# A linear attention block whose engines' instruction lists are written straight behind the launch's beginning, without a block

## The chip, the core and the metric

The kernel runs on one core of one Trainium2 chip. The metric is the device time of one execution in microseconds (us); the time of a kernel is the median of its runs.

A core has five engines, each with an instruction list of its own: TensorE (PE; its weight loads are the row PEld), VectorE (DVE), ScalarE (ACT), GpSimd (POOL) and SyncE (SP, which here only issues transfers and waits). They are held together by semaphores alone. A name with a q at its end (SPq, PEldq) is the engine's sequencer: instructions that wait, branch, drain or issue a transfer, in which the engine itself does nothing.

## What is computed

```python
B, S, D = 1, 2048, 640;  H = 32; Dh = 20
q, k, v = split(x @ wqkv)                       # per head
phi = lambda t: where(t > 0, t + 1, exp(t)) + 1e-6
pq, pk = phi(q), phi(k)
kv  = einsum("bhsd,bhse->bhde", pk, v)          # 20 x 20 per head
z   = einsum("bhsd->bhd", pk)
num = einsum("bhqd,bhde->bhqe", pq, kv)
den = einsum("bhqd,bhd->bhq", pq, z)[..., None] + 1e-6
out = (num / den).reshape(B, S, D) @ wo
```

The inputs and the output are bf16: x is 2048 x 640, wqkv 640 x 1920, wo 640 x 640.

## The kernel before

The sequence of 2048 rows is cut into 16 tiles of 128 rows, and the width of 640 into five chunks of 128. TensorE first runs six matmuls on a constant (line 269) while the first x tiles and the K weights arrive, transposes the first x tiles itself (line 194), and then makes K for all 16 tiles (line 278). From K follow phi(k), the product of phi(k) with x in two halves of the width (line 305) and, between its steps, Q (line 331). Then come the denominators (line 454), the small per-head matrices (lines 408 and 432), and the output: each tile of 128 rows is multiplied with the folded weights (line 487), evicted from PSUM by ACT (line 509) and DVE (line 512) and stored by SP (line 497). The last tile is cut in three pieces, and its last store is issued by ACT.

The kernel does not call the engines while it lays out the work. A class `Plan` records every operation with the tiles that it reads and writes (`add`), works out from these which semaphores it must wait for, and keeps one list for each engine. Only at the end does `emit(engine, handle)` write a list out: for each operation its waits, the operation, and the increment of its semaphore. So the order on each engine is fixed before a single instruction is written, and the two ends of a list are set by where `emit` is called.

Before this point the launch (line 673, where the program object is made) has already written its own beginning: POOL sets four constants in memory, and all five engines meet at an opening barrier. In it every engine drains and adds one to a semaphore (gather); POOL waits until four have done so, takes the four off again, and adds four to a second semaphore (release), of which each other engine takes one.

Behind it the kernel opens a block (`nc.Block()`, line 636) and gives it a function for each engine: SP at lines 638 to 643, POOL 645, ACT 649, DVE 653, TensorE 657. The program then has seven parts: the beginning, one for each engine and an end. The beginning ends with an unconditional branch of each engine to its own part; each part ends with a branch to the end; and the end is a second, closing barrier of all five engines, built like the opening one. All of the closing part stands under line 95, where the stack of contexts is closed.

SP's list has something more behind its last operation: a wait for each of the 17 output stores (line 643), so that the program isn't over before its output has landed. The compiler puts two such waits into one instruction; the last of them it has folded into SP's closing branch.

Of the kernel before, what the change touches and what calls it, by code (L numbers as in the profile page):

```python
# [82 lines left out]
def bass_standalone__linear_attn_block__prompt_kernel(nc, x, wqkv, wo, out):  # L83
# [11 lines left out]
    with contextlib.ExitStack() as ctx:  # L95
        es = ctx.enter_context
# [35 lines left out]
        P = Plan(nc, es)  # L132
# [370 lines left out]
        out_keys = []  # L503
# [129 lines left out]
            out_tile(st, 2 * (st % 4) if st > 5 else 2 * (st % 2))  # L633
        out_last(NT - 1, (6, 7, 0))

        block = es(nc.Block())

        @block.sync
        def _(e):
            P.emit("sp", e)  # L640
            for key in out_keys:
                op = P.writers[key]
                e.wait_ge(P.sem_obj[op.sem], op.val)

        @block.gpsimd
        def _(e):
            P.emit("pool", e)

        @block.scalar
        def _(e):  # L650
            P.emit("act", e)

        @block.vector
        def _(e):
            P.emit("dve", e)

        @block.tensor
        def _(e):
            P.emit("pe", e)


# [26 lines left out]
```

## Time and profile before

| | us |
|---|---|
| median of 3 runs | 102.03 |
| the runs | 102.68, 102.03, 101.84 |
| the profiled execution | 102.49 |
| span of the profiled execution, first to last instruction | 100.6 |
| busy: PE, DVE, ACT, POOL | 97.1, 69.3, 43.3, 3.2 |

The span counts the opening and the closing barrier. The profiled execution's own time is 1.9 us longer than its span; what fills that is not in the trace. The granted TensorE clock is 1.000 of full speed throughout.

How to read it: a row of a source line gives the sequencer's or engine's instructions of that line, their number, the least, middle and largest duration in ns, and when the first and the last of them start, in us to one decimal. A row of the timeline gives start, duration, engine, line, operation, tiles, and in brackets how long the engine had been idle and what ended that. In a table of stretches each row is a part of the span with the busy time of each engine in it.

### The profile page before, as it was taken

The page shows a single profiled execution, that of the slowest core. Times are in us where ns is not written, and L with a number is a line of the kernel's source. Part 1 is how long each engine was busy: PE and PEld are TensorE (multiplying, and loading weights), DVE is VectorE, ACT ScalarE, POOL GpSimd, SP SyncE. Part 2 cuts the span into 40 slices and gives each one's busy share as a digit, 9 for nine tenths or more (in the row PEclk, how much of TensorE's full clock was granted, in tenths as well). Part 3 has the DMA queues.
Part 4 walks back from the last instruction along what each step waited for, and adds up shares of the span by engine and source line. Part 5 has one row for each costly group of instructions (what it writes and reads, how often), then busy time and mean ns, then how long its engine had stood idle before and what let it go on. Part 6 is the DMA issues. An engine that isn't in the chain of part 4 may idle for free.

```text
span 100.6 us, 1810 instructions
## 1 busy us (share of the span) xinstructions
PE 97.1 (97%) x703; PEld 63.2 (63%) x703; DVE 69.3 (69%) x140; ACT 43.3 (43%) x76; POOL 3.2 (3%) x15
## 2 busy tenths in 40 slices
PE   6999999999999999999999999999999999999990
PEld 2567777777777666656567565755537677777770
DVE  0217998888889378899996445668899669853331
ACT  5005554445697220462132228389844531333330
POOL 6600000000000000000000000000000000000000
PEclk9999999999999999999999999999999999999999
DMA  2954989999999400000000000114440323632233
GB/s 51 330 206 92 226 173 159 173 354 372 364 358 207 76 3 0 0 3 0 7 0 0 0 0 0 31 28 122 136 119 0 130 76 103 256 131 105 99 123 130
DMA packets 17076, 11.93 MB, mean 119 GB/s; under 512 B 8749, under 2 KB 17069, under 8 KB 17069
## 3 DMA queue, kind: packets, MB, share of 16 engines
q1 hardware_dynamic: 16349, 11.14, 39.8%
q10 hardware_dynamic: 720, 0.70, 2.0%
q8 instruction: 5, 0.08, 0.4%
q14 instruction: 2, 0.02, 0.1%
HBM read 5.90 MB, written 2.62 MB: 85 GB/s over the span
## 4 chain that ended last, share of the span: by engine, by line
PE 90%; DVE 4%; ACT 2%; issue 1%
PE ps L278 22%; PE ps L487 22%; PE ps L305 22%; PE ps L331 16%; PE ps L269 3%; DVE pq L344 2%; PE ps L194 2%; PE ps L408 2%; PE ps L454 1%; ACT eq L339 1%; DVE pq L479 1%; PE ps L432 1%; DVE eq L341 1%; ACT w2g L436 1%; DVE osb L512 0%
## 5 line engine op out<-in xcount | busy, mean ns | idle before, releaser
L331 PE MATMUL ps<-xT,wqp 128*128 128x512 bf16 x100 | 24.2, 379 | 0.0
L305 PE MATMUL ps<-pk,xn 128*128 128x320 bf16 x160 | 23.5, 300 | 0.0
L278 PE MATMUL ps<-wk,xT 128*128 128x320 bf16 x160 | 22.9, 304 | 0.0
L487 PE MATMUL ps<-w2p,pq 128*128 128x320 bf16 (+1 forms) x165 | 22.1, 295 | 0.1
L339 ACT ACTIVATE eq<-ps 128x512 bf16<-128x512 f32 x20 | 12.0, 599 | 21.2 <-PE ps L331 20.7
L305 PEld LDWEIGHTS ps<-pk,xn 128*128 128x128 bf16 x160 | 15.5, 98 | 7.5 <-DVE pt L320 0.2
L487 PEld LDWEIGHTS ps<-w2p,pq 128*128 128x128 bf16 x165 | 15.7, 98 | 6.7 <-DVE pq L479 0.6
L278 PEld LDWEIGHTS ps<-wk,xT 128*128 128x128 bf16 x160 | 15.6, 99 | 6.6 <-DVE xT L199 0.3
L291 ACT ACTIVATE ek<-ps 128x640 bf16<-128x640 f32 x16 | 11.2, 704 | 14.8 <-PE ps L278 14.8
L331 PEld LDWEIGHTS ps<-xT,wqp 128*128 128x128 bf16 x100 | 9.7, 97 | 9.0
L344 DVE SCALAR_TENSOR_TENSOR pq<-ps,eq 128x512 bf16<-128x512 f32 x20 | 13.8, 692 | 0.7
L296 DVE SCALAR_TENSOR_TENSOR pk<-ps,ek 128x640 bf16<-128x640 f32 x16 | 13.2, 825 | 0.6
L512 DVE CAST osb<-ps 128x320 bf16<-128x320 f32 (+1 forms) x16 | 7.7, 480 | 7.9 <-PE ps L487 7.8
L509 ACT CAST osb<-ps 128x320 bf16<-128x320 f32 (+1 forms) x17 | 7.0, 416 | 13.4 <-PE ps L487 11.5
L341 DVE TENSOR_SCALAR eq<-eq 128x512 bf16<-128x512 bf16 x20 | 5.8, 292 | 9.8 <-ACT eq L339 9.7
L479 DVE TENSOR_TENSOR pq<-pq,rd 128x512 bf16<-128x512 bf16 x20 | 7.8, 417 | 0.7 <-DMA rd<-rdc 0.7
L293 DVE TENSOR_SCALAR ek<-ek 128x640 bf16<-128x640 bf16 x16 | 5.2, 325 | 2.0 <-ACT ek L291 1.9
L199 DVE COPY xT<-ps 128x256 bf16<-128x256 bf16 (+1 forms) x8 | 2.2, 320 | 6.2 <-PE ps L194 6.2
L350 DVE TENSOR_TENSOR za<-pk 128x1280 f32<-128x1280 bf16 x4 | 5.8, 1482 | 0.0
L350 DVE TENSOR_TENSOR za<-za 128x1280 f32<-128x1280 f32 x3 | 4.4, 1481 | 0.0
L259 ACT COPY wqp<-wqn 128x640 bf16<-128x640 bf16 x5 | 4.3, 935 | 0.0
L436 ACT CAST w2g<-ps 120x640 bf16<-120x640 f32 (+1 forms) x6 | 4.0, 690 | 0.0
(38 smaller groups left out, 33.2 us busy)
## 6 DMA issues: line engine op xcount, KB each, us to landing
out_dram<-osb SPq DMA_DIRECT2D x15, 160.0 KB, 1.8
xn<-in_x_dram SPq DMA_DIRECT2D x3, 640.0 KB, 8.0
wqn<-in_wqkv_dram SPq DMA_DIRECT2D x1, 800.0 KB, 5.5
wv<-in_wqkv_dram SPq DMA_DIRECT2D x1, 800.0 KB, 11.3
wog<-in_wo_dram SPq DMA_DIRECT2D x1, 750.0 KB, 13.2
w2p<-w2g SPq DMA_DIRECT2D x5, 150.0 KB
rd<-rdc SPq DMA_DIRECT2D x8, 64.0 KB, 2.4
wk<-in_wqkv_dram SPq DMA_DIRECT2D x3, 160.0 KB, 4.1
```

What stands on the lines that cost most here:

```text
L278: r = e.matmul(bank(b + h, HALF), xT[:, c * S + 128 * st:c * S + 128 * st + 128], wk[:, c * D + HALF * h:c * D + HALF * (h + 1)], start=(c ...
L291: P.add("act", lambda e: e.activation(fold(t[:, :]), two_banks(b), ACTF.Exp), reads=banks + ["table"], writes=[("ek", st % 3)])
L296: P.add("dve", lambda e: e.scalar_tensor_tensor(fold(pk[:, st * D:(st + 1) * D]), two_banks(b), 0.0, fold(t[:, :]), ALU.max, ALU.add), rea ...
L305: r = e.matmul(bank(d, HALF), xn[:, st * D + 128 * d:st * D + 128 * d + 128], pk[:, st * D + HALF * h:st * D + HALF * (h + 1)], start=(st ...
L331: r = e.matmul(bank(b), wqp[:, d * D + 128 * c:d * D + 128 * c + 128], xT[:, d * S + BK * sbk:d * S + BK * (sbk + 1)], start=(d == 0), sto ...
L339: P.add("act", lambda e: e.activation(t[:, :], bank(b), ACTF.Exp), reads=[("bank", b), "table"], writes=[("eq", i)])
L344: P.add("dve", lambda e: e.scalar_tensor_tensor(pq[:, c * S + BK * sbk:c * S + BK * (sbk + 1)], bank(b), 0.0, t[:, :], ALU.max, ALU.add), ...
L350: P.add("dve", lambda e: e.tensor_tensor(d_ap, a, b, ALU.add), reads=ra + rb, writes=[dst])
L479: P.add("dve", lambda e: e.tensor_tensor(v, v, rd[i][:, BK * o:BK * (o + 1)], ALU.mult), reads=[("rd", i, 2 * o), ("rd", i, 2 * o + 1), (" ...
L487: r = e.matmul(bank(b, hi - lo), pq[:, c * S + 128 * st:c * S + 128 * st + 128], w2p[:, c * D + lo:c * D + hi], start=(c == 0), stop=(c == ...
L509: P.add("act", lambda e: e.copy(osb[j][:, lo:hi], bank(b, hi - lo)), reads=[("bank", b)], writes=keys)
L512: P.add("dve", lambda e: e.tensor_copy(osb[j][:, lo:hi], bank(b, hi - lo)), reads=[("bank", b)], writes=keys)
```

## The change

The block, its five functions, the branches into and out of it and its closing barrier are gone. The five lists are written one after the other straight into the program's beginning, behind the opening barrier, TensorE's first and SP's last; SP's waits for the output stores follow its list as before. The opening barrier stays.

```diff
-        block = es(nc.Block())
-
-        @block.sync
-        def _(e):
-            P.emit("sp", e)
-            for key in out_keys:
-                op = P.writers[key]
-                e.wait_ge(P.sem_obj[op.sem], op.val)
-
-        @block.gpsimd
-        def _(e):
-            P.emit("pool", e)
-
-        @block.scalar
-        def _(e):
-            P.emit("act", e)
-
-        @block.vector
-        def _(e):
-            P.emit("dve", e)
-
-        @block.tensor
-        def _(e):
-            P.emit("pe", e)
+        P.emit("pe", nc.tensor)
+        P.emit("act", nc.scalar)
+        P.emit("dve", nc.vector)
+        P.emit("pool", nc.gpsimd)
+        P.emit("sp", nc.sync)
+        for key in out_keys:
+            op = P.writers[key]
+            nc.sync.wait_ge(P.sem_obj[op.sem], op.val)
```

On each engine the instructions from the first tile operation to the last stand in the same order in both programs. Missing from the changed one are two branches on each of the five engines, and the closing barrier's drain and semaphore instructions. SP's waits for the stores are nine instructions now, where they were eight and a branch with a wait in it.

## The prediction

> **What bounds the kernel now.** I read the page's first two lines of busy time, then the chain of waits that ended last, then the first microsecond and the last two of the timeline, and last the single source lines at both ends, because the change touches nothing but the two ends.
>
> ```profile
> span 100.6 us, 1810 instructions
> PE 97.1 (97%) x703; PEld 63.2 (63%) x703; DVE 69.3 (69%) x140; ACT 43.3 (43%) x76; POOL 3.2 (3%) x15
> PE 90%; DVE 4%; ACT 2%; issue 1%
> ```
>
> TensorE carries the span: 97.1 of 100.6 us busy and 90% of the chain. The change adds, drops and moves none of its 703 matmuls and none of the other engines' tile work. So what it can do lies where TensorE is not working, and the table of busy time by stretches shows how little that is:
>
> ```profile
> core 0: us, PE busy (x) PEld busy (x) DVE busy (x) ACT busy (x) POOL busy (x), PEclk, DMA share, GB/s
> 0.00:0.80 0.80, 0.00 (x0) 0.00 (x0) 0.00 (x0) 0.00 (x0) 0.21 (x5) 1.00 0.00 0
> 0.80:98.20 97.40, 97.15 (x703) 63.18 (x703) 68.94 (x140) 43.32 (x76) 3.04 (x11) 1.00 0.43 119
> 98.20:98.60 0.40, 0.00 (x0) 0.00 (x0) 0.32 (x1) 0.00 (x0) 0.00 (x0) 1.00 0.97 362
> 98.60:100.20 1.60, 0.00 (x0) 0.00 (x0) 0.00 (x0) 0.00 (x0) 0.00 (x0) 1.00 0.36 111
> 100.20:100.60 0.40, 0.00 (x0) 0.00 (x0) 0.00 (x0) 0.00 (x0) 0.00 (x0) 1.00 0.00 0
> ```
>
> Five stretches: the launch's beginning (0.80 us), the work (97.40), the last eviction (0.40), the last stores on their way (1.60), and 0.40 us in which no engine works and no DMA moves a byte. The middle three stay. The first and the last are the change's.
>
> **The change part by part.**
>
> (a) *The opening branches.* Each engine's list begins with one unconditional branch in the program; the changed program has none. What does one cost? The tensor engine's branch is made at line 657, SP's at line 638.
>
> ```profile
> nothing on L657; most used: ['L487', 'L278', 'L305', 'L331', 'L79', 'L454', 'L408', 'L194', 'L432', 'L339', 'L341', 'L344', 'L390', 'L479', 'L673', 'L509', 'L497', 'L291', 'L293', 'L296', 'L512', 'L269', 'L95', 'L199', 'L471']
> L673 SPq EVENT_SEMAPHORE  x1: 17/17/17, 0.7 to 0.7; - x1
> L673 PEldq EVENT_SEMAPHORE  x1: 51/51/51, 0.7 to 0.7; - x1
> 0.80 0.40 SPq L220 DMA_DIRECT2D xn<-in_x_dram  x1
> 0.81 0.14 PEld L269 LDWEIGHTS ps<-const-bfloat16-1.0 128*128 128x128 bf16 x2 [0.81 <-issue]
> ```
>
> No opening branch leaves a record, and the first instruction stands at 0.80 or 0.81 us right behind the opening barrier's release, which starts at 0.7 (0.65 to 0.75 by the rounding) and lasts 17 to 51 ns. What could be a branch is at most the gap between: 0.80 - 0.65 - 0.02 = 0.13 us on SP, at least 0. A branch that goes to the very next instruction seems to have been dropped when the program was compiled. I take 0; 0.13 us is the other end. It would count in full, because the start sets when the first x tile lands and TensorE waits for it. The Trainium skill (Advanced Engine Details and Errata, Control Flow Timing) gives some 51 ns to a branch that is always taken; by that the sum below would be 0.05 us lower, and no run here shows such a branch.
>
> That start is the only place where the branches could be hidden by anything: six warm-up matmuls run from 0.84, and TensorE then waits for the x tile.
>
> ```profile
> 0.84 2.72 PE L269 MATMUL ps<-const-bfloat16-1.0 128*128 128x512 bf16 x6 [0.84 <-PEq L673]
> PEld ps L194 <- DMA xn<-in_x_dram: 0.9, 1, 0.9
> ```
>
> The transfer ends that wait, so an earlier TensorE start alone would bring nothing; only SP's earlier DMA would. With a price of 0 for SP's branch there is nothing to cover.
>
> (b) *The closing branches and the closing barrier.* They all stand under line 95.
>
> ```profile
> L643 SPq EVENT_SEMAPHORE  x1: 28/28/28, 100.1 to 100.1; - x1
> L95 SPq COMPARE_BRANCH  x1: 33/33/33, 100.2 to 100.2; - x1
> L95 SPq DRAIN  x1: 13/13/13, 100.3 to 100.3; - x1
> L95 POOLq EVENT_SEMAPHORE  x2: 17/17/17, 100.4 to 100.5; - x2
> L95 SPq EVENT_SEMAPHORE  x1: 17/17/17, 100.5 to 100.5; - x1
> L95 PEldq EVENT_SEMAPHORE  x1: 51/51/51, 100.5 to 100.5; - x1
> SPq L95 <- PEq L95: 0.2, 1, 0.2
> ```
>
> SP's eighth and last wait for the output stores starts at 100.1 us and lasts 28 ns; asked for the stretch from 100.15 us on, the view of that line answers with nothing:
>
> ```profile
> nothing on L643; most used: ['L95']
> ```
>
> So the wait is over by 100.15 us, and not before 100.08 (100.05 and 28 ns). Behind it come, one after the other on the path that ends the program: SP's branch with one more wait folded in (100.2), SP's drain (100.3), POOL's collecting and releasing semaphore instructions (100.4 and 100.5), and the release on all five (100.5), the last of them TensorE's of 51 ns, with which the span ends at 100.6 (100.55 to 100.65). Removed from the path: 100.6 - 100.15 = 0.45 us by the rounded ends, with 0.40 us and 0.57 us as the ends of the rounding. The 1.60 us row above ends at 100.20 with stores and the next 0.40 row is empty, which says the same. I take 0.42, near the empty stretch's 0.40.
>
> The other engines' drains cost nothing, as they lie beside the stores: DVE's at 98.2, ACT's at 98.9, TensorE's at 96.2.
>
> ```profile
> L95 PEldq DRAIN  x1: 1968/1968/1968, 96.2 to 96.2; - x1
> L95 DVEq DRAIN  x1: 364/364/364, 98.2 to 98.2; - x1
> L95 ACTq DRAIN  x1: 152/152/152, 98.9 to 98.9; - x1
> ```
>
> Their cover, the stores' landing, stays: SP still waits for every output store, now with nine wait instructions for eight plus a branch with a wait. Those lie in the same order; the ninth shares the instruction that waits for ACT's last store, so it adds nothing behind it. Late next is that store, which stays the last.
>
> (c) *Order in which the lists are recorded* (TensorE first instead of SP first). Each engine's own list is the same from its first tile instruction to its last, so no queue is passed by another: nothing.
>
> (d) *What lies around the span.* The profiled execution took 102.49 us and its span is 100.6, so 1.9 us of the time are outside what the trace lists. The removed barrier ends where that part begins. I take it as unchanged, as SP, the last to arrive, arrives 0.42 us earlier and the rest follows it. Bounds: all 0.42 us may be swallowed if something else ends the run (gain 0); and if part of the 1.9 us is each engine's own, four engines now do theirs while SP waits. What cannot go is a hand-over between the engines, whose nearest row is the 0.2 us that SP waits at the closing barrier; so at most 1.9 - 0.2 = 1.7 us more.
>
> The Trainium skill (Runtime: NRT & Kernel Launch, The ~15µs preamble/postamble breakdown) says that the launch closes with a barrier of its own, about 1.5 us, in which all engines are awaited. No row here lists it; the 1.9 us outside the span leave room for it. By that rule the kernel's own barrier is done twice, and the sum stays as it stands.
>
> **The sum** is made against the profiled execution: 102.49 - 0 (a) - 0.42 (b) - 0 (c) - 0 (d) = 102.07 us. That execution stood 0.46 us above the median of the three runs (102.03; 101.84 to 102.68), so on the median's scale: 102.03 - 0.42 = **101.6 us**, 0.4% less. A measurement of this kernel tells about 1%, 1.02 us, from no change (three runs spread over 0.84 us); so this is a gain within 1%.
>
> **The rivals.**
>
> *Swallowed.* The run ends on something that the barrier does not hold up, or the launch's closing takes up later arrivals at no cost. For it: nothing in the trace shows what ends the run. Against it: SP's arrival is what all five wait for in the trace. Time: 102.0.
>
> ```profile
> 3.62 0.72 POOL L159 TENSOR_SCALAR_AFFINE_SELECT bm<-bm 128x120 bf16<-128x120 bf16 x2
> ```
>
> *More comes off than the barrier.* The four engines that are done early (TensorE and DVE at 98.2 to 98.6, ACT at 99.1, POOL, with the row above, at some 4 us) go on into the 1.9 us part at once and finish their share before SP's last store lands.
>
> For it: between that row and the span's end lie 96 us in which POOL could have done any closing work. Against it: SP has its own share, and arrives last in both programs; if all shares are alike, nothing more goes. The range is 0 to 1.7 us more; half of it gives 101.6 - 0.85 = 100.8. It is faster by over 1% once more than 1.02 - 0.42 = 0.6 us of it go.
>
> *The early engines get in the way (the other side).* An engine that runs past its list's end loads its next code by DMA. The trace has one such load behind the span, none between the last matmul and the span's end, where the engines stand at the barrier:
>
> ```profile
> q14 instruction: 1, 0.01, 0.2%
> q14 instruction: 2, 0.02, 0.1%
> out_dram<-osb SPq DMA_DIRECT2D x1, 120.0 KB, 1.7
> out_dram<-osb ACTq DMA_DIRECT2D x1, 40.0 KB, 1.5
> ```
>
> The first row is the stretch from 101 to 110 us (0.2% of 16 engines' 9 us: 0.3 us on one DMA engine), the second the whole span (0.1% of 16 times 100.6: 1.6 us for two, so 0.3 to 0.8 us each, an estimate from these rounded rows). If TensorE, DVE and ACT each load at 98.2 to 99.1, on a DMA engine that is 97% busy with the last stores, the last store lands up to 3 x 0.8 = 2.4 us later in the worst case, less 0.42: 104.0 us. One load of 0.42 us on the path makes it even; slower by over 1% it gets from 1.44 us on, so two of the long loads must fall on the same DMA engine. Against it: one load only is seen behind the span, and of 16 DMA engines it takes one.
>
> *The change does not do what it says* holds for its opening half, and is in the forecast already: there are no opening branches to remove.
>
> **How the numbers follow.** Forecast (0.42 us off, 0 to 0.13 more): 0.60. Swallowed, 102.0: 0.20. More comes off, 99.9 to 101.6: 0.15. Early engines in the way: 0.05. Faster by over 1% (below 101.0): nearly all of the third, with its upper part left out, and some weight for a lucky median: 0.14. Slower by over 1%: the fourth: 0.05. Within 1%: the rest, 0.81. The range holds the first two cases with a quarter us for a median of few runs (the three shown lie 0.19 below and 0.65 above theirs), up to 102.2, and the third down to its middle, 100.8. What is left out is half of the third, most of the fourth and a little of the first: under 2 in 10.
>
> **What would show it right or wrong.** Right: in the new profile nothing stands under line 95; SP's nine waits end the span at about 100.1 us, so the span is some 0.4 us shorter; the first DMA again starts about 0.06 to 0.1 us behind the release; and the time outside the span is again 1.9 us. If the first DMA moves forward by 0.05 us or more, (a) had a price. If the time outside the span grows by 0.4, the gain was swallowed; if it shrinks, more came off. If the last stores take longer than 1.5 and 1.7 us, the early engines got in the way. The forecast is wrong as a whole if the matmul part between 0.84 and 98.2 us changes its length.

## The result, and the profile after

| | before | changed |
|---|---|---|
| median, us | 102.48 (12 runs) | 101.59 (12 runs, 100.99 to 103.82) |
| ratio, with 95% interval | | 0.9904 [0.9877, 0.9931] |
| profiled execution, us | 102.49 | 101.73 |
| its span, us | 100.6 | 100.0 |
| its time outside the span, us | 1.9 | 1.7 |

The changed kernel is 0.9 us faster (0.7 to 1.3 by the interval): within 1%, but twice the 0.42 us that the working gave. That the forecast of 101.6 us meets the median is luck: the three runs of before that were shown had a median of 102.03, and twelve have 102.48, so a baseline 0.45 us too low made up for a gain 0.47 us too small. One run of the changed kernel, that of 103.82 us, is 2% above the others and is left out of the ratio and of the means below.

First the views that answer to those of before. The page's span and busy line, and the table of stretches of the changed kernel (first DMA, last eviction, last store as bounds):

```profile
span 100.0 us, 1793 instructions
PE 96.8 (97%) x697; PEld 63.0 (63%) x703; DVE 69.2 (69%) x140; ACT 43.3 (43%) x76; POOL 3.3 (3%) x15
```

```profile
core 0: us, PE busy (x) PEld busy (x) DVE busy (x) ACT busy (x) POOL busy (x), PEclk, DMA share, GB/s
0.00:0.80 0.80, 0.00 (x0) 0.00 (x0) 0.00 (x0) 0.00 (x0) 0.21 (x5) 1.00 0.00 0
0.80:98.06 97.26, 96.76 (x697) 62.97 (x703) 68.83 (x139) 43.34 (x76) 3.05 (x11) 1.00 0.46 119
98.06:98.42 0.36, 0.00 (x0) 0.00 (x0) 0.32 (x1) 0.00 (x0) 0.00 (x0) 1.00 0.99 370
98.42:100.00 1.58, 0.00 (x0) 0.00 (x0) 0.00 (x0) 0.00 (x0) 0.00 (x0) 1.00 0.38 119
```

The beginning is 0.80 us as before, the last stores take 1.58 us (1.60), and the fifth stretch, the empty 0.40 us, is gone. The work is 0.14 us shorter in this pair of executions (97.26 against 97.40); spans of this kernel scatter by more, 99.7 to 100.5 us over its runs. The six matmuls that are missing are records that the trace lost (697 of 703; their weight loads are all there).

Nothing stands under line 95 any more. The end by the source line of SP's waits, and the opening, where line 657 is the launch, as 673 was in before:

```profile
L643 SPq EVENT_SEMAPHORE  x9: 17/28/28, 98.4 to 100.0; - x9
```

```profile
L657 SPq EVENT_SEMAPHORE  x1: 17/17/17, 0.7 to 0.7; - x1
...
L657 PEldq EVENT_SEMAPHORE  x1: 51/51/51, 0.7 to 0.7; - x1
```

```profile
0.80 0.40 SPq L220 DMA_DIRECT2D xn<-in_x_dram  x1
0.81 1.28 ACT L229 ACT_TABLE_LOAD   x1 [0.81 <-PEq L657]
0.81 0.14 PEld L269 LDWEIGHTS ps<-const-bfloat16-1.0 128*128 128x128 bf16 x2 [0.81 <-issue]
```

SP's ninth wait, at 100.0 us, is the last instruction of the program. At the start nothing moved: release at 0.7, first DMA at 0.80, first weight load at 0.81, in both kernels.

**Where the rest of the gain is** shows only when every execution's own time is set beside its span. All runs give both. Means over the runs:

| | runs | span | outside the span | sum |
|---|---|---|---|---|
| before (runs beside the first experiments) | 31 | 100.60 | 1.82 | 102.42 |
| changed | 11 | 100.16 | 1.43 | 101.59 |
| changed, once more | 8 | 100.16 | 1.31 | 101.48 |

So 0.44 us went inside the span, and another 0.4 to 0.5 outside it. The time outside the changed kernel's span has two values: in 14 of its 19 runs it is 1.2 to 1.3 us, in five 1.7 to 1.8, near the 1.82 of before. So the part of the gain outside the span comes nearly all from the 14.

### The profile page after: what moved, and what is told of

Same layout as the page of the kernel before. It is cut to its first block, busy times and chain, and to the rows that moved or that the text cites. A ratio compares the mean times of both kernels' runs of the same rounds, so it can differ in the third digit from the quotient of the medians.

```text
span 100.0 us, 1793 instructions
## 1 busy us (share of the span) xinstructions
PE 96.8 (97%) x697; PEld 63.0 (63%) x703; DVE 69.2 (69%) x140; ACT 43.3 (43%) x76; POOL 3.3 (3%) x15
## 4 chain that ended last, share of the span: by engine, by line
PE 91%; DVE 4%; ACT 2%; issue 1%
PE ps L278 22%; PE ps L487 22%; PE ps L305 22%; PE ps L331 16%; PE ps L269 3%; DVE pq L344 2%; PE ps L194 2%; PE ps L408 2%; PE ps L454 1%; ACT eq L339 1%; DVE pq L479 1%; PE ps L432 1%; DVE eq L341 1%; ACT w2g L436 1%; DVE osb L512 0%
## 5 line engine op out<-in xcount | busy, mean ns | idle before, releaser
L331 PE MATMUL ps<-xT,wqp 128*128 128x512 bf16 x94 | 23.1, 379 | 0.3
```

The costliest lines, as they stand in the source:

```text
L331: r = e.matmul(bank(b), wqp[:, d * D + 128 * c:d * D + 128 * c + 128], xT[:, d * S + BK * sbk:d * S + BK * (sbk + 1)], start=(d == 0), sto ...
```

## The experiments

Each kernel is the changed one with the edit shown, which stands behind (or in) SP's loop of waits. The column to read is the time outside the span, which is steadier than the total (a kernel's runs hold it within 0.1 to 0.4 us, but for the two values just named, where their totals scatter by about 1). `last` stands for the semaphore of the last output store:

```python
last = P.sem_obj[P.writers[out_keys[-1]].sem]
```

| kernel | runs | total, median | ratio to before, 95% interval | span | outside |
|---|---|---|---|---|---|
| again | 8 | 101.45 | 0.9910 [0.9875, 0.9944] | 100.16 | 1.31 |
| bar1 | 12 | 102.26 | 0.9982 [0.9957, 1.0007] | 100.42 | 1.81 |
| bar2 | 12 | 102.51 | 1.0003 [0.9973, 1.0032] | 100.76 | 1.75 |
| hold4 | 12 | 102.38 | 0.9997 [0.9973, 1.0022] | 100.28 | 2.07 |
| hold_pool | 10 | 102.20 | 0.9972 [0.9945, 1.0000] | 100.13 | 2.13 |
| hold_pe | 10 | 101.98 | 0.9952 [0.9922, 0.9982] | 100.18 | 1.81 |
| hold_act | 10 | 101.79 | 0.9941 [0.9909, 0.9974] | 100.04 | 1.69 |
| hold_dve | 10 | 101.77 | 0.9953 [0.9917, 0.9990] | 100.20 | 1.67 |
| pool_mid | 10 | 102.17 | 0.9972 [0.9946, 0.9997] | 100.31 | 1.82 |
| pool_early | 4 | 101.34 | 0.9896 [0.9845, 0.9946] | 99.85 | 1.48 |
| wait_pool | 10 | 101.84 | 0.9956 [0.9923, 0.9988] | 100.11 | 1.79 |
| wait_act | 10 | 101.79 | 0.9940 [0.9913, 0.9967] | 100.31 | 1.43 |

### Is it the barrier's own time, or the early finish of four engines?

**again**: no edit.

> The changed kernel once more, beside the three below. Theory A (barrier alone): only the 0.4 us of the closing barrier and branch went; the ratio to before is about 0.996, and the time outside the span is the same in both kernels. Theory B (early finish): the time outside the span is shorter too, since four engines do their closing part while SP still waits; the ratio is again 0.990 (0.9 to 1.0 us), of which 0.4 us is span and 0.4 to 0.6 us lies outside it.

Measured: 0.9910, and 1.31 us outside against 1.82. Theory B.

**bar1**: the closing barrier back, without a block or branches.

```diff
+        nc.all_engine_barrier()
```

> The changed kernel with a closing barrier written behind SP's last wait, and without any block or branch: the change's closing part alone is undone. Theory A: span 0.3 to 0.35 us longer than without the barrier (the barrier without SP's branch), the total some 0.1 us below before. Theory B: the total comes back by 0.8 to 0.9 us, to within 0.1 us of before, half of it outside the span. Theory C (the opening branches cost 0.4 us or more): the total stays 0.4 to 0.6 us below before, because the opening is still without branches.

Measured: 102.26 us; 0.26 us more span than without the barrier, and 1.81 us outside it, the 1.82 of before. The total is 0.15 us below before, where B expected 0.1 at most, but the time outside is that of B; and C falls: the opening is without branches here and the time came back all the same. The 0.18 us of span that still lie between bar1 (100.42) and before (100.60) fit SP's closing branch, which bar1 lacks; its gap in the trace of before was from 100.2 to 100.3. The barrier in bar1's trace:

```profile
L644 POOLq EVENT_SEMAPHORE  x2: 17/17/17, 100.6 to 100.7; - x2
L644 POOLq DRAIN  x1: 409/409/409, 4.0 to 4.0; - x1
L644 PEldq DRAIN  x1: 1968/1968/1968, 96.6 to 96.6; - x1
L644 DVEq DRAIN  x1: 361/361/361, 98.6 to 98.6; - x1
L644 ACTq DRAIN  x1: 153/153/153, 99.3 to 99.3; - x1
L644 SPq DRAIN  x1: 13/13/13, 100.5 to 100.5; - x1
...
L644 PEldq EVENT_SEMAPHORE  x1: 51/51/51, 100.7 to 100.7; - x1
```

Four engines drain while the stores are still out; behind SP's drain at 100.5 only POOL's two instructions and the release follow. This is the part that the prediction counted.

**bar2**: a second barrier behind it (the same line twice).

> Two closing barriers in a row. The price of a barrier inside the span, apart from what follows on the engines' common arrival: theories A and B both expect the second one to add 0.2 to 0.35 us to the span, and nothing more to the time outside it. So by A bar2 is 0.5 to 0.7 us above the changed kernel, by B 1.1 to 1.3 us.

Measured: 0.34 us more span than bar1, and 1.75 us outside, so it adds 0.25 to 0.27 us in all. A second barrier costs its own steps and nothing else, which fits that no engine has a head start left to lose. Its rows, all within 0.3 us:

```profile
L645 SPq DRAIN  x1: 7/7/7, 101.0 to 101.0; - x1
...
L645 PEldq EVENT_SEMAPHORE  x1: 51/51/51, 101.3 to 101.3; - x1
```

**hold4**: no barrier, but nobody may finish early.

```diff
+        for e in (nc.tensor, nc.scalar, nc.vector, nc.gpsimd):
+            e.wait_ge(last, 16)
```

> No barrier; but TensorE, ACT, DVE and POOL each wait at the end of their lists for the last output store, as SP does, so that all five finish together. Nothing is collected or released. Theory A: the same time as the changed kernel within 0.1 us. Theory B: the span stays (at most 0.05 us more) and the time outside it grows back by 0.4 to 0.6 us, because no engine has a head start.

Measured: 102.38 us, the time of before, with a span of 100.28 and 2.07 us outside. The added instructions are four and take 17 to 51 ns, all beside each other:

```profile
L646 ACTq EVENT_SEMAPHORE  x1: 17/17/17, 100.6 to 100.6; - x1
L646 POOLq EVENT_SEMAPHORE  x1: 17/17/17, 100.6 to 100.6; - x1
L646 DVEq EVENT_SEMAPHORE  x1: 21/21/21, 100.6 to 100.6; - x1
L646 PEldq EVENT_SEMAPHORE  x1: 51/51/51, 100.6 to 100.6; - x1
```

This is the run that decides. Nothing is collected, handed over or released, and the gain outside the span is gone: what the changed kernel wins there needs four engines that end their lists while SP still waits. Theory A falls. The total is that of before only because 0.3 us less span meet 0.25 us more outside; by theory B the time outside should have grown by 0.4 to 0.6 us, and it grew by 0.6 to 0.8. hold4 even loses more outside the span than bar1 (2.07 against 1.81). That the barrier lets engines drain early, as the rows of bar1 show, would account for it; it was not tried.

### Which engine needs the head start?

One engine alone waits beside SP, for example

```diff
+        nc.gpsimd.wait_ge(last, 16)
```

and in the same way `nc.tensor`, `nc.scalar`, `nc.vector`.

**hold_pool**:

> As hold4, but POOL alone waits for the last output store beside SP; TensorE, ACT and DVE finish early. hold4 showed that the time outside the span goes from about 1.3 us to 2.1 us when all four are held. Theory B1 (one engine has a long closing part and sets it): one of the four kernels that hold a single engine gets the whole 2.1 us, the other three stay at 1.3. Theory B2 (the closing work is handed from engine to engine, or shared): each held engine brings a part, 0.1 to 0.3 us, to 1.4 to 1.6 us. For POOL, the slowest of the five on small things, B1 expects 2.1 us and a total of 102.3 us, B2 1.5 us and 101.7 us.

**hold_pe**:

> TensorE alone is held beside SP. B1 expects 1.3 us outside the span (2.1 us if TensorE is the long one: it has the longest list, and its release in the closing barrier took 51 ns where the others' took 17 to 21), B2 1.5 us.

**hold_act**:

> ACT alone is held beside SP; it is the last of the four to be through anyway, some 0.9 us before SP. B1 expects 1.3 us outside the span, B2 1.4 to 1.5 us.

**hold_dve**:

> DVE alone is held beside SP. B1 expects 1.3 us outside the span (2.1 us if DVE is the long one: its small instructions took longest after TensorE's, 21 ns against 17), B2 1.5 us.

Measured outside the span: POOL 2.13, TensorE 1.81, ACT 1.69, DVE 1.67 us; SP alone 1.3. Neither theory as it stood. POOL alone brings all that the four together bring (2.07), as B1 has it, but the others aren't at 1.3; and the four parts over 1.3 (0.83, 0.51, 0.39, 0.37) add up to 2.1 us, where hold4 has 0.8, so they are not handed on as B2 has it. What would fit is a third: each engine has a closing part of its own length, all run beside each other, and the one that ends last sets the end (theory M in the next runs). For ACT and DVE, and nearly for TensorE, another reading fits as well: their 1.7 and 1.8 us are the changed kernel's own second value, taken in nearly every run. Only POOL's 2.13 stands clear of it.

### Does the head start count by its length?

**pool_mid**: POOL waits for the last store but one (`out_keys[-2]` in place of `out_keys[-1]`); **pool_early**: for the store before that (`out_keys[-3]`).

> POOL waits for the last store but one, which lands some 0.27 us before the last (99.71 against 99.97 us in the changed kernel's trace). Theory M (each engine needs a closing part of its own length behind its list, all run beside each other, and the execution ends with the last): POOL's is 2.13 us, SP's 1.27, so POOL ends it, 0.27 us earlier than where it waited for the last store: 1.85 us outside the span, total 101.9. Theory W (a wait on POOL at the end costs some 0.8 us whenever it is over): 2.1 us outside, total 102.2.

> POOL waits for the store two before the last, which lands about 1.0 us before the last (98.98 against 99.97 us). Theory M: POOL's 2.13 us are over 0.1 us before SP's 1.27, so nothing is lost: 1.3 us outside the span, total 101.5, the changed kernel's. Theory W: 2.1 us outside, total 102.2.

```profile
L645 POOLq EVENT_SEMAPHORE  x1: 17/17/17, 99.7 to 99.7; - x1
```

```profile
L645 POOLq EVENT_SEMAPHORE  x1: 17/17/17, 99.1 to 99.1; - x1
```

The first row is pool_mid, with SP's last wait at 99.9 and the span's end at 100.0 us, the second pool_early, with its end at 100.1. Measured outside: 1.82 us for pool_mid (M: 1.85; W: 2.1), and for pool_early two runs at 1.3 and two at 1.7 us, the two values of the changed kernel, with a total of 101.34. With some 0.3 us of head start POOL's closing part still sets the end, by just that much less; with 1.0 us, in the four runs there are, it does not show. W falls and M's figures come out; but 1.82 us lies close to the second value (1.7 to 1.8), so the total alone does not prove M.

**wait_pool** and **wait_act**: another engine does SP's waits, and SP is done early.

```diff
-            nc.sync.wait_ge(P.sem_obj[op.sem], op.val)
+            nc.gpsimd.wait_ge(P.sem_obj[op.sem], op.val)
```

(wait_act: `nc.scalar`.)

> The waits for the 17 stores move from SP to POOL, so SP is done at 98.4 us and POOL is the last. Theory M: POOL's 2.13 us set it, 2.1 us outside the span, total 102.2, as where both waited. Theory S (the head start of most engines counts, not which one is last): 1.3 us outside, total 101.5.

> The waits move from SP to ACT. Theory M: ACT's closing part, 1.7 us from the run that held it, sets it: 1.7 us outside the span, total 101.8 to 101.9, 0.3 to 0.4 us over the changed kernel. Theory S: 1.3 us outside, total 101.5.

Measured outside: 1.79 us with POOL last (M 2.1, S 1.3) and 1.43 with ACT last (M 1.7, S 1.3). Both theories miss. POOL last costs 0.4 us more than SP last, against S; but POOL's and ACT's times are 0.34 and 0.26 us shorter than where SP was late beside them, against a plain M. So the closing parts are not wholly independent. One thing goes with it: in the profiled executions of these two kernels no code load (one packet of 8 KB on the DMA queue for instructions) lies behind the span, while there is one whenever SP was among the last (hold_pool, hold_act and nine others), except in the one of again. The changed kernel's profiled execution had it, with 1.73 us outside the span, and again's did not, with 1.28. The stretches from 100 us on (changed) and from 99.6 us on (again):

```profile
q14 instruction: 1, 0.01, 0.3%
```

```profile
DMA packets 0, 0.00 MB, mean 0 GB/s; under 512 B 0, under 2 KB 0, under 8 KB 0
```

The trace of before shows what this load has to do with the time. Its load lies in the stretch from 102 to 103 us, in the twentieth of forty slices:

```profile
DMA  0000000000000000000700000000000000000000
q14 instruction: 1, 0.01, 1.9%
```

So it starts at 102.48 to 102.50 us, and it takes 1.9% of 16 DMA engines' 1 us, which is 0.30 us; it lands at about 102.80. The reported time of that execution is 102.49 us, 0.30 less, and 0.30 us is where POOL sets the first constant:

```profile
0.30 0.10 POOL L673 MEMSET const-float32-0.0<- 128x1 f32 x1 [0.30 <-issue]
```

The same sum for all eleven profiled executions with a load, from their traces (us; the span's end is the end of its last instruction):

| kernel | load starts, behind the span | load lands, less the start of the first constant | reported time | outside |
|---|---|---|---|---|
| before | 1.93 | 102.49 | 102.49 | 1.93 |
| changed | 1.56 | 101.73 | 101.73 | 1.73 |
| pool_early | 1.57 | 101.75 | 101.75 | 1.65 |
| hold_act | 1.55 | 101.08 | 101.08 | 1.57 |
| hold_dve | 1.52 | 101.44 | 101.44 | 1.75 |
| hold_pe | 1.68 | 102.18 | 102.17 | 1.88 |
| pool_mid | 1.68 | 101.83 | 101.83 | 1.87 |
| hold_pool | 1.95 | 102.19 | 102.19 | 2.10 |
| hold4 | 1.92 | 102.74 | 102.74 | 2.13 |
| bar1 | 1.64 | 102.62 | 102.62 | 1.86 |
| bar2 | 1.06 | 102.59 | 103.09 | 1.77 |

In ten of the eleven the reported time ends, to 0.01 us, where the load lands, counted from the first constant. So the 1.9 us outside the span of before are not wholly missing from the trace, as was said ahead of the prediction: they are the time up to this load, which no row fills, and the load itself (0.3 to 0.55 us in the eleven), less the 0.30 us. In again, without it, 1.28 us are left, the first of the changed kernel's two values. That its other runs divide in the same way is an inference, as one trace of each kernel is kept.

The table also corrects theory M. With ACT or DVE held, the load starts 1.55 and 1.52 us behind the span, as in the changed kernel and pool_early: in these traces the two do not delay it, and their 1.7 us is the second value. TensorE delays it by 0.1 us and POOL by 0.4. POOL's is the clean case: in pool_mid the load starts 1.68 us behind the span and, as POOL's wait was through 0.27 us before it, 1.95 us behind POOL, the same as in hold_pool. What stays open: which engine's load it is, why a held ACT or DVE seems to bring it in nearly every run, why it starts earlier behind a barrier written by hand (bar1, bar2), and what ends the executions without it. No run changed the load alone.

No kernel here clearly beats the changed one. POOL is the wrong engine to be last (1.79 us outside); ACT (1.43) is not told apart from SP, whose 19 runs have a mean of 1.38.

## Why the prediction was right or wrong, point by point

(a) *Opening branches at 0*: right. The first DMA starts at 0.80 us in both kernels, 0.1 us behind the release, and bar1, which has no opening branches, is as slow as before but for the 0.18 us of span that SP's closing branch can explain.

(b) *Closing barrier and branch at 0.42 us*: right, 0.44 us of span over 11 and 31 runs. The nine waits, the place of the last and the landing of the last stores (1.5 and 1.7 us again) came out as said.

(c) *Order of recording at nothing*: right as far as the runs show; the spans differ by the closing part alone.

(d) *The time outside the span unchanged*: wrong, and with it the size of the gain. The step that failed is "SP, the last to arrive, arrives 0.42 us earlier and the rest follows it". It took SP's arrival for the one that counts. The runs show that the others' count too: with SP alone late the time outside is 1.3 us in 14 of 19 runs, with DVE or ACT late beside it 1.7, with TensorE 1.8, with POOL 2.1. In before the barrier holds all of them to the end, and 1.82 us go by outside; in the changed kernel's trace POOL is through 96 us before SP, TensorE and DVE 1.6 us or more, ACT 1.2. For POOL the size is shown in the traces too: held to the end, it makes the load start 1.95 us behind the span and not 1.56. For the others the runs show that a late end costs, and not why.

The part also said that the 1.9 us lie "outside what the trace lists", and *swallowed* that "nothing in the trace shows what ends the run". Both overlook a row: the code load that the fourth rival quotes lands at 102.80 us, which is 102.49 us, the reported time, behind the first constant.

The rival that held is the second, *more comes off than the barrier*. It had the mechanism, and argued against it that "if all shares are alike, nothing more goes"; they are not alike, as POOL shows. Its middle of 0.85 us was too much, the measured 0.4 to 0.5 lies below it; with a chance of 0.15 it was held for too unlikely. *Swallowed* and *the early engines get in the way* fall: the time outside shrank, and the last stores landed as fast as before.

The sentence on the launch's own closing barrier (the Trainium skill, Runtime: NRT & Kernel Launch, The ~15µs preamble/postamble breakdown) gives 1.5 us to a wait for all engines; no row here shows that barrier, and the 1.3 to 2.1 us outside the span are only of its size. The conclusion drawn from it, that the sum stays as it stands, was mine and was wrong: what each engine does ahead of such a wait can be done early.

## What to carry to other kernels

A barrier at the very end can cost more than its own instructions: here 0.44 us were its steps with SP's branch, and about as much again lay outside the span, because engines that had long been done were held to the end. When a change touches the end of a program, set each execution's time beside its span, and look in the DMA view for what lies behind the span: here a code load ended the reported time. Let the engine that waits for the last stores be one whose late end costs little, here SP rather than POOL, with the others free to finish. A branch that left no record cost nothing that these runs show.

## What the runs showed of the hardware

The time outside the span depends on which engines end late: about 1.3 us for SP alone (1.7 in five of 19 runs), and, each beside SP, 1.7 us for DVE and ACT, 1.8 for TensorE and 2.1 for POOL. In ten of eleven profiled executions with a code load behind the span, the reported time ends with that load's landing, to 0.01 us; the load starts 1.95 us behind POOL's last wait where POOL is held, and 1.52 to 1.57 us behind the span where SP, ACT or DVE is the last. A second all-engine barrier on idle engines cost 0.25 to 0.27 us. A single wait of 17 ns on POOL, put where it ends with the last store, cost 0.6 to 0.8 us of the execution (102.20 against 101.45 us; 0.9972 against 0.9910 of before); the same wait about 1 us earlier cost nothing that four runs show (101.34).
